# Linear attention into a soft mixture of experts: loads joined into longer rows, output chunks moved among the half-1 products

## The chip, the cores and the metric

The kernel runs on one core of a Trainium2 chip. The metric is device time in microseconds of one execution. Five engines work side by side, each through its own list of instructions in order: TensorE (PE in the profile; PEld is its loading of weights), VectorE (DVE), ScalarE (ACT), GpSimd (POOL) and SyncE (SP), which here only issues DMAs. They wait for each other by semaphores. Data comes from HBM into SBUF (128 partitions) and goes back by 16 DMA engines, which all queues share.

## The reference

```python
def _attn_ref(q, k, v, g_norm):                  # all (8, 8, 576, 64)
    kv = np.einsum('bhsd,bhse->bhde', k, v)
    out = np.einsum('bhsd,bhde->bhse', q, kv)
    rms = np.sqrt(np.mean(out * out, axis=-1, keepdims=True) + 1e-06)
    return (out / rms * g_norm).astype(np.float32)

def _moe_ref(x, phi, w1, w2):                    # x (4608, 512), phi (512, 32), w1 (8, 512, 1024), w2 (8, 1024, 512)
    logits = x @ phi
    d = softmax over the tokens of logits        # written out with max, exp and sum
    slot_input = (d.T @ x).reshape(E, S_per_e, D)
    for e in range(E):
        h = np.maximum(slot_input[e] @ w1[e], 0.0)
        slot_out[e] = h @ w2[e]
    c = softmax over the slots of logits
    return (c @ slot_out.reshape(n_slots, D)).astype(np.float32)
```

x is the attention's result, laid out as 4608 tokens by 512 (8 heads by 64). There are 8 experts with 4 slots each. Everything is float32: 62 MB come in and 9.4 MB go out.

## The kernel before

**Memory.** One tile, `arena`, holds 160 KB of every partition. What is loaded gets a place in it, counted in KB per partition: `KV_AT[b]` for the keys and values of batch b (18 KB), `Q_AT[g]` for the queries of batches 2g and 2g+1 (18 KB), `W_AT` for the sixteen weight units (16 KB each; `w1` 7 lies in `xall` instead, and `w2` 2 in two halves). Places are used again: a load into a place waits until the last reader of what lay there is done. Outputs are put together in the arena too.

**Loads.** All loads and stores are issued by SP, in program order, and run in one hardware queue. At the start (L107 to L119) the kernel issues kv0, the constants, q0 and kv1 in pieces, then kv2, q1 (8 KB), kv3, q1 (10 KB), kv4 and q2. A DMA's semaphore is taken by the eighth-next DMA, which waits for it. `loads_behind` (L122) issues kv5, kv6, q3, kv7 after token tile 9, four weight units after tile 18, three after 27, one after 31; the others are issued between the later stages (L519 to L521, L665 to L674).

**Token loop.** There are 36 tiles T of 128 tokens. Nine tiles make a group of two batches. `kv_step(b, i)` forms the products of keys and values of batch b in three steps, ahead of the first tile that needs them: for b from 2 up, steps 0, 1 and 2 come before the query products of the three tiles ahead of that batch's first tile, so batch 2 (first tile 9) starts ahead of tile 6, batch 4 ahead of tile 15. Each tile then has `products` (TensorE, query by block-diagonal key-value matrix `bd`), `square` and `evict` (ACT), mean squares and root (DVE, ACT), scaling (POOL), logits (DVE), and `group_sum`, the softmax-weighted sum of the tokens (TensorE). `fill` issues matmuls of zeros at the start and behind the loop, on TensorE, whose results nothing reads.

**Experts.** Behind the loop the slots' inputs are transposed, and `expert_h(e)` (weights w1) and `expert_y(e, hf)` (weights w2) run on TensorE. The output's columns are made in two halves `hf`. For experts 2 to 7 a w2 unit holds one half for two experts: units 2, 3, 4 serve half 0, units 5, 6, 7 half 1.

**Output.** `gather(hf)` copies the summed products out of PSUM, `mix(hf)` adds the four partial sums by one matmul and copies the result to `z`, and `output(hf, k, f)` makes one of six chunks of a half: eight matmuls (four for each of two PSUM tiles), a copy by ACT (L655), a copy by DVE (L657), and one store of 768 KB (L658). Half-1 outputs need every half-1 product; half-0 outputs need half 0 alone. TensorE follows the written order of L680 to L700.

Of the kernel before, what the change touches and what calls it, by code (L numbers as in the profile page):

```python
# [14 lines left out]
P = 128  # L15
B, H, S, D = 8, 8, 576, 64
NPAIR = H // 2
NS = 32
NE = 8
# [8 lines left out]
NX = 14  # L28
EARLY = (18, 2, 0)
LATE_FILL = (21, 5, 5, 2, 2)  # L30
TOK = 4608
UNIT = 4096
KB = 256
ARENA = 160 * KB
LATE = 6
KV_AT = (0, 36, 54, 90, 108, 0, 18, 36)
Q_AT = (18, 72, 142, 54)
W_AT = {
# [3 lines left out]
}  # L42
SCRATCH = 1024
EPS_RMS = 1e-6
# [3 lines left out]
@with_exitstack  # L48
def soft_moe_linear_attention(ctx: ExitStack, tc: tile.TileContext, kv_in, q_in, w1_in, w2_in, c_in, out):


    nc = tc.nc
# [11 lines left out]
    def place(at, n):  # L64
        return arena[:, at * KB : at * KB + n]

    def load_kv(b, g=None):
        lo, hi = (0, TOK) if g is None else (2304 * g, 2304 * g + 2304)
        nc.sync.dma_start(place(KV_AT[b], TOK)[:, lo:hi], kv_in[b, :, lo:hi])

    def load_q(g, half=None):
        lo, hi = {None: (0, TOK), 0: (0, 2048), 1: (2048, TOK)}[half]
        nc.sync.dma_start(place(Q_AT[g], TOK)[:, lo:hi], q_in[g, :, lo:hi])

# [13 lines left out]
    def homes(kind, u):  # L88
        at = W_AT[kind, u]
        if at is None:  # L90
            return [xflat[:, :UNIT]]
        return [place(a, UNIT // len(at)) for a in at]

    def load_w(kind, u):
        parts = homes(kind, u)
        n = UNIT // len(parts)
        for i, t in enumerate(parts):
            nc.sync.dma_start(t, (w1_in if kind == "w1" else w2_in)[u, :, i * n : i * n + n])

    def w_block(kind, u, i):  # L100
# [4 lines left out]


    load_kv(0, 0)  # L107
    nc.sync.dma_start(cst, c_in)
    load_kv(0, 1)
    load_q(0, 0)  # L110
    load_kv(1, 0)
    load_kv(1, 1)
    load_q(0, 1)
    load_kv(2)
    load_q(1, 0)
    load_kv(3)
    load_q(1, 1)
    load_kv(4)
    load_q(2)  # L119


    loads_behind = {  # L122
        9: lambda: (load_kv(5), load_kv(6), load_q(3), load_kv(7)),
        18: lambda: [load_w(k, e) for e in range(2) for k in ("w1", "w2")],
        27: lambda: [load_w("w1", e) for e in range(2, 5)],
        31: lambda: load_w("w1", 5),
    }
# [308 lines left out]

    fill(EARLY[0])

    for g in range(2):
        kv = Kv(0, "o" if g else "kv", 2 if g else None)  # L440
        kv.products(2 * g)
        kv.products(2 * g + 1)
        kv.borders((g,))
        kv.slots((g,))
        fill(EARLY[1 + g])
    T_at, diag_at, pb_at, d_at, sums_at = {}, {}, {}, {}, {}
# [70 lines left out]
    for i in todo_sums:  # L517
        group_sum(*i)
    load_w("w1", 6)  # L519
    load_w("w1", 7)  # L520
    load_w("w2", 2)  # L521
    fill(LATE_FILL[0], home=ps.tile([P, 512], F32, tag="m", name="fill"), cols=512)
# [88 lines left out]
    def expert_y(e, hf):  # L611
        u, at = w2_unit(e, hf)
        for c in range(8):
            j = c % 4
            nc.tensor.matmul(  # L615
                pY[32 * j : 32 * j + 32, hf, :256],
                lhsT=hTs[e][:, c],
                rhs=w_block("w2", u, at + c),
                start=e == 0 and c < 4,
                stop=e == NE - 1 and c >= 4,  # L620
            )
# [42 lines left out]
    expert_h(0)  # L664
    load_w("w2", 3)  # L665
    expert_h(1)
    halves(0)
    load_w("w2", 4)
    load_w("w2", 5)
    combine(0)  # L670
    expert_h(2)
    halves(1)
    load_w("w2", 6)
    load_w("w2", 7)  # L674
    combine(1)
# [7 lines left out]
    gather(0)  # L683
    expert_y(2, 1)
    mix(0)
    expert_y(3, 1)
    output(0, *chunks[0])
    output(0, *chunks[1])
    expert_y(4, 1)
    expert_y(5, 1)  # L690
    output(0, *chunks[2])
    output(0, *chunks[3])
    expert_y(6, 1)
    expert_y(7, 1)
    gather(1)
    output(0, *chunks[4])
    mix(1)
    output(0, *chunks[5])
    for k, f in chunks:
# [3 lines left out]
def build_program():  # L703
    import concourse.bacc as bacc

    nc = bacc.Bacc("TRN2", target_bir_lowering=False, num_devices=1, dynamic_dma_scratch_size=SCRATCH)
    shapes = {"kv": (B, P, TOK), "qt": (B // 2, P, TOK), "w1": (NE, P, UNIT), "w2": (NE, P, UNIT), "cs": (P, 129)}
    args = [nc.dram_tensor(f"in_{n}_dram", s, F32, kind="ExternalInput").ap() for n, s in shapes.items()]
    args.append(nc.dram_tensor("out_0_dram", (2, NCH, P, 2, 4 * CT * NS), F32, kind="ExternalOutput").ap())
    with tile.TileContext(nc, schedule_with_timeline_sim=True) as tc, tc.manual_schedule():  # L710
        soft_moe_linear_attention(tc, *args)
    return nc
# [43 lines left out]
```

## Time and profile before

| | |
|---|---|
| median of 3 runs | 176.16 us (176.01 to 177.61) |
| the profiled execution, its own time | 175.97 us |
| span of that execution in the profile | 174.2 us |
| PE busy | 148.2 us (85%) |
| DVE, ACT, POOL busy | 88.3, 86.8, 55.7 us |
| read from HBM, written | 61.93 MB, 9.44 MB |
| DMA packets | 6645, 71.68 MB, mean 411 GB/s |

The span runs from the first instruction to the last; the execution's own time holds what lies around it as well. Busy time of an engine is a mean over stages that have different limits, so the stages are read one by one: the token loop from about 12 to 103 us, the softmax's end to 116, the experts to 139, the outputs from 144. A row of the timeline gives start, length, engine, line, operation, output and inputs with shapes, the count of instructions in it, and in brackets how long the engine had stood idle before it and what released it. "DMA to landing" is the time from a DMA's issue to its semaphore.

### The profile page before, as it was taken

Reading aid. Unit: us, or ns where it says so; the run is one execution under the profiler, and the core shown is the slowest. Engines: PE = TensorE matmul, PEld = TensorE weight load, DVE = VectorE, ACT = ScalarE, POOL = GpSimd, SP = SyncE. Lnnn points to the kernel's source line nnn. Section 1 sums busy time; section 2 is a strip of 40 time slices with the busy share of each in tenths; the row PEclk is TensorE's granted clock in tenths of the full one; section 3 lists DMA queues with packets and bytes.
Section 4 is the critical chain, followed back from the end, with each engine's and each line's share of the span. In section 5 each row is a group of like instructions: output and inputs, shape, how many; then the busy total and the mean of one; then the engine's idle time right before and its main releaser. Section 6 shows DMA issues by size and latency. Waiting matters only on the chain.

```text
span 174.2 us, 4772 instructions
## 1 busy us (share of the span) xinstructions
PE 148.2 (85%) x2024; PEld 108.9 (63%) x2024; DVE 88.3 (51%) x180; ACT 86.8 (50%) x224; POOL 55.7 (32%) x65
## 2 busy tenths in 40 slices
PE   7577799999989899999999769989999959989500
PEld 5456778889779788888996555456556424445200
DVE  1122156566486565466663778733888114457600
ACT  2036286986957957878779553102234003336400
POOL 6000067656546676266773568000000000000000
PEclk9999999999999999999999999999999999999955
DMA  5999999999999999999999999999999999999994
GB/s 188 416 429 426 439 414 432 420 432 440 414 432 423 421 431 420 420 427 436 429 418 419 433 418 433 429 429 406 440 421 419 425 425 426 386 398 406 419 419 199
DMA packets 6645, 71.68 MB, mean 411 GB/s; under 512 B 736, under 2 KB 864, under 8 KB 2400
## 3 DMA queue, kind: packets, MB, share of 16 engines
q1 hardware_dynamic: 6624, 71.37, 97.5%
q8 instruction: 16, 0.26, 0.6%
q14 instruction: 5, 0.04, 0.1%
HBM read 61.93 MB, written 9.44 MB: 410 GB/s over the span
## 4 chain that ended last, share of the span: by engine, by line
PE 46%; DMA 20%; ACT 11%; DVE 11%; issue 3%; POOL 2%; SPq 1%; POOLq 0%; DVEq 0%
PE o L252 17%; DMA arena<-in_w_dram 11%; DMA arena<-in_kv_dram 9%; PE kvp_kv L184 8%; PE po L647 5%; PE pY L615 4%; PE ph L597 3%; DVE logits L329 3%; PE pS L386 2%; DVE ms L275 2%; ACT arena L655 2%; POOL part L324 2%; ACT bd L219 2%; PE o L243 2%; ACT sq L262 2%
## 5 line engine op out<-in xcount | busy, mean ns | idle before, releaser
L252 PE MATMUL o<-bd,arena 128*128 128x192 f32 x256 | 49.4, 336 | 1.4 <-ACT xall L270 0.6
L252 PEld LDWEIGHTS o<-bd,arena 128*128 128x128 f32 x256 | 40.8, 190 | 4.7 <-ACT xall L270 1.6
L302 POOL TENSOR_TENSOR xall<-xall,r 128x512 f32<-128x512 f32 x34 | 34.8, 1044 | 0.0
L324 POOL TENSOR_TENSOR part<-part,r 128x512 f32<-128x512 f32 x17 | 17.8, 1049 | 51.5 <-DVE r L293 51.5
L329 DVE TENSOR_REDUCE logits<-part 128x64 f32<-128x512 f32 (+1 forms) x19 | 19.3, 1015 | 16.1 <-POOL part L324 16.0
L275 DVE TENSOR_REDUCE ms<-sq 128x16 f32<-128x1024 f32 (+1 forms) x19 | 22.0, 1156 | 6.2 <-ACT sq L262 6.2
L262 ACT ACTIVATE sq<-o 128x512 f32<-128x512 f32 x36 | 21.5, 596 | 6.5 <-PE o L252 5.9
L270 ACT COPY xall<-o 128x512 f32<-128x512 f32 x34 | 20.6, 607 | 0.0
L184 PE MATMUL kvp_kv<-arena 128*64 128x64 f32 x480 | 17.3, 225 | 3.6 <-DMA arena<-in_kv_dram 3.6
L655 ACT COPY arena<-po 128x768 f32<-128x768 f32 x12 | 9.3, 800 | 20.2 <-DMA arena<-in_w_dram 10.3
L184 PEld LDWEIGHTS kvp_kv<-arena 128*64 128x64 f32 x480 | 15.2, 138 | 6.5 <-DMA arena<-in_kv_dram 4.5
L615 PE MATMUL pY<-arena,xall 128*32 128x256 f32 x256 | 15.2, 380 | 2.4 <-DMA arena<-in_w_dram 2.4
L657 DVE COPY arena<-po 128x768 f32<-128x768 f32 x12 | 11.3, 956 | 8.0 <-PE po L647 7.2
L647 PE MATMUL po<-logits,z 32*128 32x384 f32 x96 | 13.7, 526 | 1.6 <-ACT arena L655 1.0
L615 PEld LDWEIGHTS pY<-arena,xall 128*32 128x32 f32 x256 | 8.0, 110 | 9.1 <-issue 3.2
L597 PE MATMUL ph<-arena,sTe 128*32 128x256 f32 x224 | 12.7, 379 | 0.3 <-DVE sTe L544 0.3
L269 ACT COPY part<-o 128x256 f32<-128x256 f32 x34 | 12.6, 371 | 0.0
L386 PE MATMUL pS<-xall,d 128*32 128x129 f32 x288 | 10.7, 276 | 2.1 <-ACT d L374 2.1
L283 ACT ACTIVATE r<-ms,eps 128x16 f32<-128x16 f32 x17 | 5.2, 308 | 12.8 <-DVE ms L275 12.6
L647 PEld LDWEIGHTS po<-logits,z 32*128 32x128 f32 x96 | 6.3, 183 | 8.2 <-ACT arena L655 4.1
L291 DVE SCALAR_TENSOR_TENSOR r<-ms,r 128x16 f32<-128x16 f32 x17 | 3.0, 175 | 15.3 <-ACT r L284 15.3
L597 PEld LDWEIGHTS ph<-arena,sTe 128*32 128x32 f32 x224 | 7.2, 110 | 5.2 <-DVE sTe L544 0.6
(88 smaller groups left out, 143.9 us busy)
## 6 DMA issues: line engine op xcount, KB each, us to landing
arena<-in_w_dram SPq DMA_DIRECT2D x14, 2048.0 KB, 20.7
arena<-in_kv_dram SPq DMA_DIRECT2D x6, 2304.0 KB, 30.4
out_dram<-arena SPq DMA_DIRECT2D x12, 768.0 KB, 6.5
arena<-in_kv_dram SPq DMA_DIRECT2D x4, 1152.0 KB, 10.1
arena<-in_qt_dram SPq DMA_DIRECT2D x2, 2304.0 KB, 32.1
arena<-in_qt_dram SPq DMA_DIRECT2D x2, 1280.0 KB, 23.2
arena<-in_qt_dram SPq DMA_DIRECT2D x2, 1024.0 KB, 16.4
xall<-in_w_dram SPq DMA_DIRECT2D x1, 2048.0 KB, 15.4
```

The costliest lines, as they stand in the source:

```text
L184: nc.tensor.matmul(self.pkv[lo : lo + 64, w, g], lhsT=main[:, w, 1, c, lo : lo + 64], rhs=main[:, w, 0, c, lo : lo + 64], start=c == 0 and ...
L252: nc.tensor.matmul(o[:, r, :192], lhsT=q_main(2 * g + i)[:, r, at : at + P], rhs=bds[i][:, r], start=True, stop=True)
L262: nc.scalar.activation(sqs[s][:, T - starts[s]], o[:, :, 32:160], AF.Square, scale=0.125)
L270: nc.scalar.copy(xts[T % NX][:, :, :128], o[:, :, 32:160])
L275: nc.vector.tensor_reduce(out=mss[s], in_=sqs.pop(s).rearrange("p t j (w d) -> p (t j w) d", w=2), axis=AX.X, op=ALU.add)
L302: nc.gpsimd.tensor_tensor(out=x, in0=x, in1=r[:, i].rearrange("p (j w) -> p j w", w=2).unsqueeze(3).to_broadcast([P, 4, 2, D]), op=ALU.mult,)
L324: engine.tensor_tensor(out=part, in0=part, in1=rs_of[s].unsqueeze(3).to_broadcast([P, STAGES[s], H, NS]), op=ALU.mult)
L329: nc.vector.tensor_reduce(out=L[:, pos(starts[s]) : pos(starts[s]) + STAGES[s]], in_=parts.pop(s).rearrange("p t h n -> p t n h"), axis=AX ...
L386: nc.tensor.matmul(pS[32 * j : 32 * j + 32], lhsT=ds[G][:, i], rhs=x[:, j], start=i == 0, stop=i == GROUPS[G] - 1)
L597: nc.tensor.matmul(ph[32 * j : 32 * j + 32], lhsT=sTe[:, (4 * e + c) * NS : (4 * e + c + 1) * NS], rhs=w_block("w1", e, 4 * c + j), start= ...
L615: nc.tensor.matmul(pY[32 * j : 32 * j + 32, hf, :256], lhsT=hTs[e][:, c], rhs=w_block("w2", u, at + c), start=e == 0 and c < 4, stop=e == ...
L647: nc.tensor.matmul(po[:, u, : CT * NS].rearrange("p (g x) -> p g x", g=2), lhsT=z[lo : lo + 32, f * P : (f + 1) * P], rhs=cT[k][lo : lo + 32],
```

## The change

The places in the arena are laid out anew so that what is loaded one after the other lies side by side, and such loads become one DMA with a longer row per partition. The arrays in HBM are put together by the host to match.

- kv0, q0 and kv1 are loaded as before, in the same pieces and order (`load_head`).
- `t1`: kv2 and q1 in one row of 36 KB. It is issued at the start, in the place of kv2.
- kv3 alone (18 KB). It now lies where kv0 lay, and is issued behind the first batch's products in program order.
- `t2`: kv4, q2 and kv5 in one row of 54 KB, issued behind kv3.
- `t3`: kv6, q3 and kv7 in one row of 54 KB, after tile 9.
- Weight units w1 0 with w2 0, w1 1 with w2 1, w1 3 with w1 4 and w2 5 with w2 6 become rows of 32 KB; the other units stay single. The second pair is issued after tile 21 instead of 18.
- The fills at the start have 512 columns instead of 256, and half the count.
- At the end, half-0 chunks 0 and 1 stand ahead of the first two pending half-1 products, chunk 2 ahead of the next two, chunks 3 and 4 ahead of the last two, and chunk 5 between `gather(1)` and `mix(1)`.

```diff
-EARLY = (18, 2, 0)
+EARLY = (9, 1, 0)
...
-KV_AT = (0, 36, 54, 90, 108, 0, 18, 36)
-Q_AT = (18, 72, 142, 54)
+KV_AT = (0, 36, 54, 0, 90, 126, 18, 54)
+Q_AT = (18, 72, 108, 36)
 W_AT = {
-    ("w1", 0): (72,), ("w2", 0): (88,), ("w1", 1): (104,), ("w2", 1): (120,), ("w1", 2): (136,),
-    ("w1", 3): (0,), ("w1", 4): (16,), ("w1", 5): (32,), ("w1", 6): (48,), ("w1", 7): None,
-    ("w2", 2): (64, 152), ("w2", 3): (72,), ("w2", 4): (88,), ("w2", 5): (104,), ("w2", 6): (120,), ("w2", 7): (136,),
+    ("w1", 0): (72,), ("w2", 0): (88,), ("w1", 1): (128,), ("w2", 1): (144,), ("w1", 2): (104,),
+    ("w1", 3): (0,), ("w1", 4): (16,), ("w1", 5): (56,), ("w1", 6): (40,), ("w1", 7): None,
+    ("w2", 2): (32, 120), ("w2", 3): (72,), ("w2", 4): (88,), ("w2", 5): (128,), ("w2", 6): (144,), ("w2", 7): (104,),
 }
+W_ROWS = (2, 2, 1, 2, 1, 1, 1, 1, 1, 1, 2, 1)
+W_ORDER = [("w1", 0), ("w2", 0), ("w1", 1), ("w2", 1)] + [("w1", e) for e in range(2, NE)] + [("w2", u) for u in range(2, NE)]
...
+    def load_head(u, lo, hi):
+        at = (KV_AT[0], KV_AT[1], Q_AT[0])[u]
+        nc.sync.dma_start(place(at, TOK)[:, lo:hi], head_in[u, :, lo:hi])
+
+    def load_row(at, src):
+        nc.sync.dma_start(place(at, src.shape[-1]), src)
...
-    def load_w(kind, u):
-        parts = homes(kind, u)
-        n = UNIT // len(parts)
+    def load_w(*units):
+        lo = W_ORDER.index(units[0])
+        n = UNIT * len(units)
+        row = w_in[:, lo * UNIT * P : (lo * UNIT * P) + n * P].rearrange("o (p n) -> (o p) n", p=P)
+        parts = homes(*units[0])
+        if len(units) > 1:
+            parts = [place(W_AT[units[0]][0], n)]
         for i, t in enumerate(parts):
-            nc.sync.dma_start(t, (w1_in if kind == "w1" else w2_in)[u, :, i * n : i * n + n])
+            m = n // len(parts)
+            nc.sync.dma_start(t, row[:, i * m : i * m + m])
...
-    load_kv(0, 0)
+    load_head(0, 0, 2304)
     nc.sync.dma_start(cst, c_in)
-    load_kv(0, 1)
-    load_q(0, 0)
-    load_kv(1, 0)
-    load_kv(1, 1)
-    load_q(0, 1)
-    load_kv(2)
-    load_q(1, 0)
-    load_kv(3)
-    load_q(1, 1)
-    load_kv(4)
-    load_q(2)
+    load_head(0, 2304, TOK)
+    load_head(2, 0, 2048)
+    load_head(1, 0, 2304)
+    load_head(1, 2304, TOK)
+    load_head(2, 2048, TOK)
+    load_row(KV_AT[2], t1_in)
...
     loads_behind = {
-        9: lambda: (load_kv(5), load_kv(6), load_q(3), load_kv(7)),
-        18: lambda: [load_w(k, e) for e in range(2) for k in ("w1", "w2")],
-        27: lambda: [load_w("w1", e) for e in range(2, 5)],
-        31: lambda: load_w("w1", 5),
+        9: lambda: load_row(KV_AT[6], t3_in),
+        18: lambda: load_w(("w1", 0), ("w2", 0)),
+        21: lambda: load_w(("w1", 1), ("w2", 1)),
+        27: lambda: (load_w(("w1", 2)), load_w(("w1", 3), ("w1", 4))),
+        31: lambda: load_w(("w1", 5)),
     }
...
-    fill(EARLY[0])
+    fill(EARLY[0], cols=512)
...
-        fill(EARLY[1 + g])
+        fill(EARLY[1 + g], cols=512)
+    load_row(KV_AT[3], kv3_in)
+    load_row(KV_AT[4], t2_in)
...
     halves(0)
-    load_w("w2", 4)
-    load_w("w2", 5)
+    load_w(("w2", 4))
     combine(0)
     expert_h(2)
     halves(1)
-    load_w("w2", 6)
-    load_w("w2", 7)
+    load_w(("w2", 5), ("w2", 6))
+    load_w(("w2", 7))
...
     gather(0)
-    expert_y(2, 1)
     mix(0)
-    expert_y(3, 1)
     output(0, *chunks[0])
     output(0, *chunks[1])
+    expert_y(2, 1)
+    expert_y(3, 1)
+    output(0, *chunks[2])
     expert_y(4, 1)
     expert_y(5, 1)
-    output(0, *chunks[2])
     output(0, *chunks[3])
+    output(0, *chunks[4])
     expert_y(6, 1)
     expert_y(7, 1)
     gather(1)
-    output(0, *chunks[4])
+    output(0, *chunks[5])
     mix(1)
-    output(0, *chunks[5])
     for k, f in chunks:
         output(1, k, f)
...
+        "in_t1_dram": np.concatenate([kv[2], qm[1]], axis=1),
+        "in_kv3_dram": kv[3],
+        "in_t2_dram": np.concatenate([kv[4], qm[2], kv[5]], axis=1),
+        "in_t3_dram": np.concatenate([kv[6], qm[3], kv[7]], axis=1),
+        "in_w_dram": np.concatenate(rows)[None],
```

More of the change, by code (lines that the diff above doesn't have):

```diff
@@ L48, in soft_moe_linear_attention @@
 @with_exitstack
-def soft_moe_linear_attention(ctx: ExitStack, tc: tile.TileContext, kv_in, q_in, w1_in, w2_in, c_in, out):
+def soft_moe_linear_attention(ctx: ExitStack, tc: tile.TileContext, head_in, t1_in, kv3_in, t2_in, t3_in, w_in, c_in, out):
     nc = tc.nc
@@ L65, in place @@
         return arena[:, at * KB : at * KB + n]
[L67 to L73, printed above, removed]
+    def load_head(u, lo, hi):
[3 more added lines that the diff above has]
+        nc.sync.dma_start(place(at, src.shape[-1]), src)
     def kv_main(b, g):
@@ L518, in soft_moe_linear_attention @@
         group_sum(*i)
-    load_w("w1", 6)
-    load_w("w1", 7)
-    load_w("w2", 2)
+    load_w(("w1", 6))
+    load_w(("w1", 7))
+    load_w(("w2", 2))
     fill(LATE_FILL[0], home=ps.tile([P, 512], F32, tag="m", name="fill"), cols=512)
@@ L664, in soft_moe_linear_attention @@
     expert_h(0)
-    load_w("w2", 3)
+    load_w(("w2", 3))
     expert_h(1)
     halves(0)
-    load_w("w2", 4)
-    load_w("w2", 5)
+    load_w(("w2", 4))
     combine(0)
@@ L706, in build_program @@
     nc = bacc.Bacc("TRN2", target_bir_lowering=False, num_devices=1, dynamic_dma_scratch_size=SCRATCH)
-    shapes = {"kv": (B, P, TOK), "qt": (B // 2, P, TOK), "w1": (NE, P, UNIT), "w2": (NE, P, UNIT), "cs": (P, 129)}
+    shapes = {
+        "head": (3, P, TOK), "t1": (P, 2 * TOK), "kv3": (P, TOK), "t2": (P, 3 * TOK), "t3": (P, 3 * TOK),
+        "w": (1, 2 * NE * P * UNIT), "cs": (P, 129),
+    }
     args = [nc.dram_tensor(f"in_{n}_dram", s, F32, kind="ExternalInput").ap() for n, s in shapes.items()]
@@ L743 @@
     cs = np.concatenate([ph, np.concatenate([g_norm, g_norm])[:, None]], axis=1)
-    arrays = {
-        "in_kv_dram": kv.reshape(B, P, TOK),
-        "in_qt_dram": qm,
-        "in_w1_dram": np.ascontiguousarray(w1),
-        "in_w2_dram": np.ascontiguousarray(w2),
+    kv = kv.reshape(B, P, TOK)
+    w = {("w1", e): w1[e] for e in range(NE)} | {("w2", u): w2[u] for u in range(NE)}
+    rows, u = [], 0
+    for n in W_ROWS:
+        rows.append(np.concatenate([w[k] for k in W_ORDER[u : u + n]], axis=1).reshape(-1))
+        u += n
+    arrays = {
+        "in_head_dram": np.stack([kv[0], kv[1], qm[0]]),
+        "in_t1_dram": np.concatenate([kv[2], qm[1]], axis=1),
[3 more added lines that the diff above has]
+        "in_w_dram": np.concatenate(rows)[None],
         "in_cs_dram": np.ascontiguousarray(cs),
```

## The prediction

> **What bounds the kernel now.** I read the page's header first, then the windows by stage, then the timeline where one stage hands over to the next. Windows rows: stretch, length, then busy time (x instructions) of PE, PEld, DVE, ACT and POOL, granted clock, DMA share, GB/s.
>
> ```profile
> span 174.2 us, 4772 instructions
> ```
> ```profile
> 27.00:103.00 76.00, 73.82 (x1023) 63.05 (x1022) 46.60 (x91) 57.52 (x160) 45.79 (x45) 1.00 1.01 427
> 116.40:139.10 22.70, 22.64 (x416) 13.40 (x416) 13.04 (x32) 5.22 (x11) 0.00 (x0) 1.00 1.01 422
> 147.00:158.00 11.00, 10.24 (x114) 5.11 (x106) 5.69 (x8) 3.80 (x5) 0.00 (x0) 1.00 0.96 395
> ```
>
> Two things are full at once. The DMA is busy from the first microseconds to the end, at 422 to 427 GB/s, and a little less (0.96) where the outputs begin. TensorE is full too in the token loop: 73.82 of the 76 us from 27 to 103, so whatever delays it there comes back with at most 2.2 us recovered. The end belongs to the DMA: the last output store is issued at 164.7 and lands 8.5 later, at 173.2, and 1.0 us after that the span ends.
>
> ```profile
> L658 SPq DMA_DIRECT2D out_dram<-arena x1: 644/644/644, 164.7 to 164.7; - x1
> ...
> DMA to landing us min/median/max: 8.5/8.5/8.5
> ```
>
> So the last stores wait in a queue behind others: compute is ahead of the stores at the end. That lead is what a delay of compute has to eat first, and I work it out below.
>
> **Fewer, longer rows.** Loads other than the constants go from 33 to 23 DMAs, the bytes stay. In rows per DMA engine (128 partitions over 16 engines, 8 rows a DMA) 80 rows go. The nearest rows for the price of a row are the stores' 6 KB rows and the loads' 10 to 18 KB rows:
>
> ```profile
> 20.00:72.00 52.00, 50.67 (x671) 43.45 (x672) 30.91 (x60) 40.11 (x112) 30.53 (x30) 1.00 1.01 426
> 160.00:171.00 11.00, 3.44 (x24) 1.42 (x20) 3.67 (x4) 2.91 (x4) 0.00 (x0) 0.72 1.01 420
> ```
>
> An engine moves 6144 B in 6144x16/420 = 234 ns and 18432 B in 692 ns; the straight line through both leaves 5 ns for a row without bytes. 80 x 5 ns = 0.4 us off the DMA's time (ends: 0 if the 420 is due to stores being stores, 0.8 if a row costs double that; no row here is longer than 18 KB, so a loss of the same 0.4 isn't excluded). This is the whole gain of the joining, if the DMA stays the bound.
>
> **What the joining makes later.** A joined load has one landing for all it holds. kv2 and q1 are now one load, t1; kv4, q2 and kv5 are t2; kv6, q3 and kv7 are t3. kv2 before is issued at 4.5 and lands 22.4 later, at 26.9, and TensorE takes it at once:
>
> ```profile
> L69 SPq DMA_DIRECT2D arena<-in_kv_dram x1: 495/495/495, 4.5 to 4.5; - x1
> ...
> DMA to landing us min/median/max: 22.4/22.4/22.4
> ```
> ```profile
> 27.02 1.01 PEld L184 LDWEIGHTS kvp_kv<-arena 128*64 128x64 f32 x32 [0.23 <-DMA arena<-in_kv_dram]
> 27.03 1.15 PE L184 MATMUL kvp_kv<-arena 128*64 128x64 f32 x32
> ...
> 50.27 1.15 PE L184 MATMUL kvp_kv<-arena 128*64 128x64 f32 x32
> ```
>
> The row at 27 is step 0 of batch 2, ahead of tile 6 (the one at 50.3 is batch 4's). It waited 0.23 us for that landing, so it has no slack. The queue ahead of t1 is unchanged (kv0, q0, kv1 in the same six pieces), so t1 lands later than kv2 by the time of q1's 2304 KB: 2.36 MB at 427 GB/s = 5.5 us, at 32.4. TensorE runs in program order, so tiles 6 and up, and ACT, DVE and POOL behind them, start 5.4 us later. t2 lands 72 KB a partition (9.44 MB, 22.1 us) behind t1, at 54.5, where batch 4's products come at 50.3 before and 55.7 after: no second wait. t3 lands where kv7 did, near 71, for batch 6, nine tiles behind batch 4: nothing. kv3, now loaded into kv0's place, is issued once kv0's products are done, with t1 queued until 32: nothing.
>
> From 27 on the shift X = 5.4 holds, less up to 0.5 (half a microsecond of ACT waits that might close; I take 0).
>
> The loads behind the loop wait on SP for TensorE's reads and move by X too. Their slack is the queue still to run: the tightest is the w2 unit 3, issued after the first expert.
>
> ```profile
> L98 SPq DMA_DIRECT2D arena<-in_w_dram x1: 327/327/327, 118.4 to 118.4; - x1
> ...
> DMA to landing us min/median/max: 13.2/13.2/13.2
> ```
>
> It lands at 131.6, of which its own 2.1 MB at 422 GB/s are 5.0: the queue before it runs until about 126.6, 8.2 us after its issue. At X = 5.4 the issue is 2.8 us ahead still. Costed at nothing; above X of about 7 (8.2 less the 1.2 that an issue takes, below) the DMA runs dry here.
>
> **The output stage.** The experts' chain (22.64 of 22.7 busy) passes X on, and the last half-0 product ends at E = 133.68 + 5.36 + X = 139.04 + X. From there the new order is output chunk by chunk; its pieces are in the timeline of before:
>
> ```profile
> 133.68 5.36 PE L615 MATMUL pY<-arena,xall 128*32 128x256 f32 x96
> 141.48 1.07 PE L615 MATMUL pY<-arena,xall 128*32 128x256 f32 x16 [2.44 <-DMA arena<-in_w_dram]
> 142.48 0.70 PE L635 MATMUL pz<-y,sel 128*128 128x256 f32 x2
> 144.11 1.56 PE L647 MATMUL po<-logits,z 32*128 32x384 f32 x12
> 146.77 1.93 PE L615 MATMUL pY<-arena,xall 128*32 128x256 f32 x32
> 148.63 1.56 PE L647 MATMUL po<-logits,z 32*128 32x384 f32 x12
> 153.15 0.93 PE L647 MATMUL po<-logits,z 32*128 32x384 f32 x8
> 154.01 0.70 PE L635 MATMUL pz<-y,sel 128*128 128x256 f32 x2
> ```
> ```profile
> 139.11 0.42 DVE L631 COPY y<-pY 128x256 f32<-128x256 f32 x1 [3.83 <-PE pY L615]
> 143.22 0.43 DVE L637 COPY z<-pz 128x256 f32<-128x256 f32 x1 [3.68 <-PE pz L635]
> 153.29 0.42 DVE L631 COPY y<-pY 128x256 f32<-128x256 f32 x1 [0.93 <-PE pY L615]
> ```
> ```profile
> 146.15 19.23 SPq L658 DMA_DIRECT2D out_dram<-arena  x12
> ```
>
> Gather ends at E + 0.49; pz starts 0.3 later (153.71 to 154.01) and is 0.70 long; z 0.47; 0.3 again to the first chunk: E + 2.26. In before a product pair stood between gather and mix and hid them; in the new order nothing does, but that pair also waited 2.44 us for its weights, which have landed now. Two chunks take 2.66 (144.11 to 146.77), a product pair 1.86 (146.77 to 148.63), one chunk 0.75 before the next work can start. Chunks 0 and 1, pair, chunk 2, pair, chunks 3 and 4, pair: 2.26 + 2.66 + 1.86 + 0.75 + 1.86 + 2.66 + 1.86 = E + 13.9. Then chunk 5, whose last copy, DVE's, ends 2.0 later (just ahead of its store: 144.11 to 146.15) at 15.9; z of half 1 behind that copy to 16.3, chunk 6 at 16.6, and its store 2.04 behind: E + 18.6 = 157.6 + X. The pieces are measured; their new order is good to about 0.7.
>
> No store of half 1 can go before that. Six stores of 786 KB at 420 GB/s are 6 x 1.87 = 11.2 us, and the first needs some time from issue to first byte. The nearest row is the very first load's:
>
> ```profile
> L69 SPq DMA_DIRECT2D arena<-in_kv_dram x1: 371/371/371, 0.7 to 0.7; - x1
> ...
> DMA to landing us min/median/max: 5.5/5.5/5.5
> ```
>
> Its 1.18 MB at 426 GB/s are 2.8 of the 5.5 us, which leaves 2.7; the ends are 0 and 2.7. I take 1.2, below the middle, as the queue is awake by then. The last landing is then not before 157.6 + X + 12.4 = 170.0 + X. The DMA's own end is 173.2 - 0.4 = 172.8. So up to X = 2.8 compute is hidden and the change gains 0.4; beyond, each microsecond counts in full. X = 5.4 gives 175.4 for the landing.
>
> **The clock.** TensorE now stands still for 5.4 us at tile 6. Rows of PE alone (stretch, length, busy, granted clock, DMA share, GB/s):
>
> ```profile
> 137.43:140.85 3.42, 1.61 (x32) 1.00 1.01 426
> 161.33:164.74 3.41, 2.15 (x18) 1.00 1.02 423
> 164.74:168.15 3.41, 0.00 (x0) 0.50 1.01 418
> ```
> ```profile
> 1.05 3.71 PE L429 MATMUL fill<-zeros 128*128 128x256 bf16 x18 [1.05 <-DVE zeros L136]
> ...
> 109.67 1.24 PE L429 MATMUL fill<-zeros 128*128 128x512 bf16 x5
> ```
>
> The stretch with half its time busy keeps 1.00; the empty one is at 0.50. A gap of 5.4 us leaves at least 2.7 of some 3.4 us stretch empty, which is nearer to the empty row. Half clock is not free: the first fills took 206 ns for 256 columns, later ones 124 (248 for 512), so the spell at the start lasted nearly the 3.7 us of the fills. After the restart a spell of the same kind loses half its length, at most 1.9 us; 0 if the clock holds. I take 1.2, as the restart falls somewhere inside a stretch. So X = 6.6, under the 7 of the dry queue.
>
> The Trainium skill, "TensorE: Matmul & The Clock Gate", Part 1, says that one idle window of about 3.4 us, free-running, halves the clock. By that rule 5.4 us of idle contain a whole window in (5.4 - 3.4)/3.4 = 59% of placements, an estimate; the drop after the row with 2.15 us busy speaks for less idle being enough.
>
> **The sum.** Landing 170.0 + 6.6 = 176.6, span + 1.0 = 177.6. The profiled execution took 175.97 for a span of 174.2, 1.8 more, so 179.4; the median of the runs, 176.16, is 0.2 above it: 179.6. The other fills (9 of 512 columns for 18 of 256) move the same columns and cost nothing.
>
> **The rivals.**
> - The clock holds. For it, the row at 1.00 with half its time empty; against it, that more is empty here. 178.4.
> - Not slower: the late t1 is absorbed before chunk 6, so X there is under 2.8 and the DMA's queue still sets the end: 176.16 - 0.4 = 175.8, at best 175.3. For it, the 2.2 us that TensorE idles in the loop and the chunks sent ahead; against it, 5.4 less 2.2 is still 3.2, and those idles are waits in the same chain. It decides below X = 2.8.
> - Dry queue: X above 7 (a clock spell of 1.9 or a second late landing, t2 for batch 4 with under 1.2 us to spare). Then w2 arrives late as well, and half-1 products wait: 181 to 183.
> - Faster: longer rows gain more than 5 ns each and the 0.96 stretch closes (0.4 us): 174.3 or below. The DMA share of 1.01 nearly everywhere leaves no room.
>
> **How the numbers follow.** Forecast (late t1 and a clock spell) 0.43, 178.6 to 180.8; clock holds 0.25, 177.4 to 179.2; absorbed 0.20, 175.3 to 177; dry queue 0.07; faster 0.05. The range from 175.4 to 180.8 leaves out the last two and a little of the absorbed case, under 2 in 10. A measurement of this kernel tells about 1% from no change: below 174.4 is faster, above 177.9 slower. Slower: 0.43 + 0.07 + four fifths of 0.25, 0.69, rounded to 0.68; same: the rest of the clock case and the absorbed case, 0.26; faster 0.06.
>
> **What would show it.** Right: a wait of the kv products on the t1 load of some 5 us at tile 6, at 32; clock below 1.00 in the stretch behind it; the loop's end near 109 instead of 103; half-0 products ending near 145; stretches of DMA share well under 0.96 between 150 and 165; the first half-1 store issued near 164. Wrong: kv products of batch 2 starting before 30, or the loop ending at 103 to 105, or DMA share at 1.0 through the output stage with an end at 172.8. Also wrong is the row price, if stretches of 54 KB rows move less than 426 or over 430 GB/s.

## The result and the profile after

The changed kernel takes 182.33 us (median of 6 runs, 181.5 to 183.35) beside 176.83 us for the kernel before on the same chip (6 runs, 176.01 to 177.70): a ratio of 1.031, 95% interval 1.026 to 1.037. It is slower, as forecast, but by 2.7 us more than forecast, and outside the range given. The profiled execution took 182.17 us, for a span of 180.3; predicted was a span of 177.6.

From the page of the changed kernel: its span, then the granted clock and the DMA's share in 40 slices of 4.5 us.

```profile
span 180.3 us, 4735 instructions
...
PEclk9999998599999999999999999999999999999975
DMA  6999999999999999999889997999999999998993
```

There is one notch in the clock, in slices 7 and 8 (from 27 us on), and several in the DMA's row, behind the middle. TensorE's timeline of the changed kernel has what lies in the notch, and where the loop ends:

```profile
32.42 1.98 PE L186 MATMUL kvp_kv<-arena 128*64 128x64 f32 x32 [5.59 <-DMA arena<-in_t_dram]
34.33 2.72 PE L254 MATMUL o<-bd,arena 128*128 128x192 f32 x8
...
108.88 1.55 PE L254 MATMUL o<-bd,arena 128*128 128x192 f32 x8
```

Batch 2's products wait 5.59 us for t1 and start at 32.42, 5.4 later than before. They and the eight products behind them run long: 1.98 us for what takes 1.15, and 2.72 for what takes 1.55 at the loop's end. The last tile's products start at 108.88, where the kernel before has them at 101.50 (its row stands further down, in the table): a shift X of 7.4 us. The windows cut where the clock changes (stretch, length, busy time of PE, PEld, DVE, ACT and POOL, granted clock, DMA share, GB/s):

```profile
26.46:29.87 3.41, 0.37 (x3) 0.07 (x1) 2.15 (x4) 2.19 (x6) 2.94 (x3) 1.00 0.85 362
29.87:33.28 3.41, 0.85 (x16) 0.86 (x18) 1.49 (x5) 0.52 (x2) 1.86 (x3) 0.50 1.00 422
33.28:36.70 3.42, 3.42 (x29) 3.30 (x26) 0.87 (x2) 0.00 (x0) 1.30 (x2) 0.50 1.18 507
36.70:40.10 3.40, 3.40 (x61) 3.02 (x61) 0.00 (x0) 1.77 (x5) 0.00 (x0) 1.00 1.15 499
```

The half clock lasts two stretches of 3.41 us. TensorE works in it from 32.42 to 36.70, 4.3 us, and half of that is lost: 2.1 us, which with the 5.4 makes X to a tenth.

Late in the loop and behind it the DMA runs dry at times. These are windows of the changed kernel, then of the kernel before, over the same stretches:

```profile
84.00:92.00 8.00, 8.00 (x128) 6.79 (x124) 4.55 (x12) 7.15 (x20) 4.41 (x5) 1.00 0.86 321
...
106.00:114.00 8.00, 5.69 (x73) 4.74 (x72) 5.74 (x17) 5.24 (x16) 5.54 (x6) 1.00 0.83 309
...
124.00:132.00 8.00, 8.00 (x152) 4.81 (x148) 3.77 (x10) 1.97 (x4) 0.00 (x0) 1.00 0.96 369
...
158.00:168.00 10.00, 8.50 (x82) 3.81 (x78) 5.92 (x8) 3.84 (x6) 0.00 (x0) 1.00 0.91 372
```
```profile
84.00:92.00 8.00, 8.00 (x122) 7.41 (x124) 5.28 (x8) 5.64 (x17) 5.38 (x6) 1.00 1.01 426
...
106.00:114.00 8.00, 7.44 (x73) 3.71 (x65) 6.53 (x15) 1.30 (x5) 2.05 (x3) 1.00 1.01 428
...
124.00:132.00 8.00, 8.00 (x156) 4.83 (x152) 6.53 (x15) 2.19 (x6) 0.00 (x0) 1.00 1.01 422
...
158.00:168.00 10.00, 5.08 (x38) 2.24 (x32) 5.30 (x6) 4.00 (x5) 0.00 (x0) 0.84 1.01 418
```

Against the rates of before the four stretches lose 8 x (1 - 321/426) = 2.0, 2.2, 1.0 and 1.1 us of DMA time, 6.3 in all, about what the span grew by (6.1). That sum is tempting and, as the experiments show, it is not the reason: nothing on TensorE waits for what comes late in the first three of them. The end hangs on the first half-1 store. Its issue and the last store's, each with the time to its landing:

```profile
L662 SPq DMA_DIRECT2D out_dram<-arena x1: 332/332/332, 164.8 to 164.8; - x1
...
DMA to landing us min/median/max: 5.2/5.2/5.2
```
```profile
L662 SPq DMA_DIRECT2D out_dram<-arena x1: 751/751/751, 171.2 to 171.2; - x1
...
DMA to landing us min/median/max: 8.1/8.1/8.1
```

The first is issued at 164.8, which is 157.6 + X less 0.2: the chain of TensorE was forecast well. The last lands at 179.3, 14.5 later, where the prediction had 12.4. The windows of the changed kernel behind that issue say why:

```profile
164.80:168.00 3.20, 2.84 (x24) 1.21 (x22) 2.29 (x3) 1.71 (x3) 0.00 (x0) 1.00 0.90 358
168.00:172.00 4.00, 2.07 (x14) 0.82 (x12) 2.32 (x3) 1.87 (x3) 0.00 (x0) 1.00 1.01 413
172.00:176.00 4.00, 0.00 (x0) 0.00 (x0) 0.00 (x0) 0.00 (x0) 0.00 (x0) 0.65 1.02 419
176.00:179.30 3.30, 0.00 (x0) 0.00 (x0) 0.00 (x0) 0.00 (x0) 0.00 (x0) 0.50 0.38 155
```

Length by rate, they move 5.0 MB: the six stores (4.7) and 0.3 left of earlier ones. All of it at 420 GB/s would take 11.9 us. The first stretch, with the queue nearly empty, loses 3.2 x (1 - 358/420) = 0.5. The last moves 0.51 MB, 1.2 us of work for sixteen engines, in 3.3: some engines are done and the slowest is not, which costs 2.1. A landing is that of the slowest engine (the last section of this document has the row: over the last 2.3 us the engines' mean busy share is 0.12, two of sixteen on average).

### The profile page after: what moved, and what is told of

Its sections match the earlier page's. It is cut to its first block, busy times and chain, and to the rows that moved or that the text cites. A ratio compares the mean times of both kernels' runs of the same rounds, so it can differ in the third digit from the quotient of the medians.

```text
span 180.3 us, 4735 instructions
## 1 busy us (share of the span) xinstructions
PE 151.9 (84%) x2014; PEld 110.6 (61%) x2014; DVE 88.3 (49%) x180; ACT 87.0 (48%) x224; POOL 55.7 (31%) x65
## 4 chain that ended last, share of the span: by engine, by line
PE 41%; DMA 27%; DVE 11%; ACT 8%; issue 2%; SPq 2%; POOL 2%; POOLq 0%; DVEq 0%
DMA arena<-in_t_dram 15%; PE o L254 15%; DMA arena<-in_w_dram 10%; PE kvp_kv L186 8%; PE pY L619 5%; PE po L651 3%; PE ph L601 3%; DVE logits L331 3%; DVE arena L661 2%; PE pS L388 2%; DVE ms L277 2%; DMA out_dram<-arena 2%; POOL part L326 2%; SPq L71 2%; ACT bd L221 1%
## 5 line engine op out<-in xcount | busy, mean ns | idle before, releaser
L254 PE MATMUL o<-bd,arena 128*128 128x192 f32 x256 | 50.4, 341 | 1.9 <-ACT bd L231 0.8
L254 PEld LDWEIGHTS o<-bd,arena 128*128 128x128 f32 x256 | 41.9, 194 | 5.0 <-ACT xall L272 1.6
L326 POOL TENSOR_TENSOR part<-part,r 128x512 f32<-128x512 f32 x17 | 17.8, 1049 | 58.8 <-DVE r L295 58.8
L264 ACT ACTIVATE sq<-o 128x512 f32<-128x512 f32 x36 | 21.5, 596 | 14.3 <-PE o L254 13.9
L186 PE MATMUL kvp_kv<-arena 128*64 128x64 f32 x480 | 18.7, 237 | 6.8 <-DMA arena<-in_t_dram 5.6
L186 PEld LDWEIGHTS kvp_kv<-arena 128*64 128x64 f32 x480 | 16.7, 149 | 10.3 <-DMA arena<-in_t_dram 5.9
L651 PEld LDWEIGHTS po<-logits,z 32*128 32x128 f32 x96 | 5.8, 183 | 9.4 <-ACT arena L659 5.0
L431 PE MATMUL fill<-zeros 128*128 128x512 bf16 x31 | 9.4, 461 | 1.1 <-DVE zeros L138 1.1
```

The lines of the kernel that those rows point to most:

```text
L186: nc.tensor.matmul(self.pkv[lo : lo + 64, w, g], lhsT=main[:, w, 1, c, lo : lo + 64], rhs=main[:, w, 0, c, lo : lo + 64], start=c == 0 and ...
L254: nc.tensor.matmul(o[:, r, :192], lhsT=q_main(2 * g + i)[:, r, at : at + P], rhs=bds[i][:, r], start=True, stop=True)
L264: nc.scalar.activation(sqs[s][:, T - starts[s]], o[:, :, 32:160], AF.Square, scale=0.125)
L326: engine.tensor_tensor(out=part, in0=part, in1=rs_of[s].unsqueeze(3).to_broadcast([P, STAGES[s], H, NS]), op=ALU.mult)
L651: nc.tensor.matmul(po[:, u, : CT * NS].rearrange("p (g x) -> p g x", g=2), lhsT=z[lo : lo + 32, f * P : (f + 1) * P], rhs=cT[k][lo : lo + 32],
```

## The experiments

What was to be told apart: that late landings hold TensorE up, and the first half-1 store is late with it; that the DMA's dry queue costs by itself; and that the new order, the new places or the longer rows cost something. The table has, for every kernel, the start of the last tile's products (T35), the issue of the first half-1 store (S), the last landing (Z), from the timelines and the rows of DMA issues, all in us, and the ratio to the kernel before.

| kernel | T35 | S | S - T35 | Z - S | span | ratio (95%) |
|---|---|---|---|---|---|---|
| before | 101.5 | 158.8 | 57.3 | 14.4 | 174.2 | 1 |
| changed | 108.9 | 164.8 | 55.9 | 14.5 | 180.3 | 1.031 (1.026 to 1.037) |
| t1 in two | 107.2 | 162.9 | 55.7 | 14.0 | 177.9 | 1.015 (1.009 to 1.021) |
| before with t1 | 109.0 | 165.2 | 56.2 | 14.4 | 180.8 | 1.028 (1.022 to 1.034) |
| before with the new order | 101.4 | 157.7 | 56.3 | 15.7 | 174.3 | 0.994 (0.991 to 0.997) |
| changed, TensorE kept busy | 107.0 | 162.7 | 55.7 | 14.4 | 178.2 | 1.019 (1.011 to 1.026) |
| before, held up by 5 us | 106.6 | 162.0 | 55.4 | 13.4 | 176.4 | 1.010 (1.004 to 1.016) |
| before, held up by 7 us | 108.8 | 164.2 | 55.4 | 13.7 | 178.8 | 1.022 (1.016 to 1.028) |
| changed, old order | 108.9 | 171.1 | 62.2 | 14.6 | 186.8 | 1.061 (1.054 to 1.068) |
| the same, w2 5 and 6 apart | 109.7 | 165.1 | 55.4 | 14.5 | 180.7 | 1.032 (1.026 to 1.038) |
| t1 and t2 in two | 103.1 | 159.3 | 56.2 | 13.9 | 174.1 | 0.997 (0.993 to 1.000) |
| the same, kv3 earlier | 101.7 | 161.1 | 59.5 | 14.3 | 176.3 | 1.006 (1.002 to 1.009) |
| the same, w2 5 and 6 apart | 101.4 | 157.2 | 55.9 | 15.7 | 173.8 | 0.997 (0.993 to 1.000) |
| before, another execution | 101.9 | 160.7 | 58.8 | 14.5 | 176.1 | one run |

The columns S - T35 and Z - S carry the case. S follows T35 by 55.4 to 56.3 us in every kernel but four, and in those four TensorE waited for a weight in the output stage. Z follows S by 13.4 to 14.6 in every kernel but two, and those two are the ones where S is earliest (157.2 and 157.7) and the DMA's queue, not TensorE, sets the end, at 172.9 and 173.4.

**t1 in two.** Alone kv2 should come when it used to.

```diff
-    load_row(KV_AT[2], t1_in)
+    load_row(KV_AT[2], t1_in[:, :TOK])
+    load_row(Q_AT[1], t1_in[:, TOK:])
```

> The changed kernel with kv2 and q1 as two loads of 18 KB rows again, all else as changed. Theory (the late landing of t1 carries the loss): kv2's products start at 27, the clock stays at 1.00, no window of the loop under 1.0 of DMA share, ratio to the kernel before 0.99 to 1.005. Rival (long rows, the new places or the new order cost by themselves): ratio 1.015 to 1.03 although tile 6 is on time.

Half the loss went (1.015), not all of it: the theory's range is missed, and the ratio lies at the lower edge of the rival's, for a reason that neither named. Batch 2 is in time now (its products start at 27.7), and the wait stands at batch 4 instead, whose keys and values lie in t2. The timeline and the windows of this kernel:

```profile
54.60 1.98 PE L187 MATMUL kvp_kv<-arena 128*64 128x64 f32 x32 [2.67 <-DMA arena<-in_t_dram]
```
```profile
50.79:54.20 3.41, 0.87 (x24) 1.00 0.95 405
54.20:57.61 3.41, 3.01 (x35) 0.51 0.86 373
```

(The windows show PE alone.) In the changed kernel nothing waits for t2, because TensorE is already behind by then: the second late landing was hidden by the first. Here the wait costs its 2.7 us and half of a stretch at half clock besides.

**t1 alone, in the kernel before.** The converse: the old arena, order and loads, with kv2 and q1 in one row.

```diff
-    load_kv(2)
-    load_q(1, 0)
-    load_kv(3)
-    load_q(1, 1)
+    nc.sync.dma_start(place(KV_AT[2], 2 * TOK), t1_in)
+    load_kv(3)
```

> The kernel before with one edit, kv2 and q1 in one load. Theory: kv2's products wait until 32.4, the clock falls for a spell, the loop ends near 110.5 and the ratio is 1.02 to 1.035, all or nearly all of the change's loss. Rival (the loss comes from the other joins or from the order): ratio under 1.01.

1.028 of the 1.031, with the 5.28 us wait at 32.57 and the same half clock. This one join is enough for nearly the whole loss.

**t1 and t2 in two.** Both late landings undone; all else of the change stays.

```diff
-    load_row(KV_AT[2], t1_in)
+    load_row(KV_AT[2], t1_in[:, :TOK])
+    load_row(Q_AT[1], t1_in[:, TOK:])
...
-    load_row(KV_AT[4], t2_in)
+    load_row(KV_AT[4], t2_in[:, :TOK])
+    load_row(Q_AT[2], t2_in[:, TOK:])
```

> The changed kernel with kv2 apart from q1 and kv4 apart from q2 and kv5, so that neither batch's keys and values wait for their neighbours; t3, the rows of two weight units, the places and the order stay. Theory: tiles 6 and 15 are on time, clock 1.00 behind the start, DMA share 1.00 or more from 84 to 132, ratio 0.99 to 1.0. Rival (the weights' rows and places or t3 cost too): ratio 1.005 or more, with the queue dry somewhere behind the loop.

The ratio is 0.997 (0.993 to 1.000), and the clock stays at 1.00. Together the two landings are the whole loss, within the noise. A smaller one shows now: 0.87 us of waiting for kv3 at 38.3, which the kernel before loaded ahead of the second part of q1 and this one behind all of it.

**The shift by itself.** To see what a hold-up of TensorE costs without any joined load, matmuls of zeros whose results nothing reads were put ahead of tile 6, 24 and 33 of 512 columns, in the kernel before; and 24 in the changed kernel, where they fill the wait for t1 and keep the clock up.

```diff
+        if T == 6:
+            fill(24, home=ps.tile([P, 512], F32, tag="m", name="fill"), cols=512)
         for b in range(1, B):
```

> The changed kernel with 24 fills of 512 columns on TensorE while it waits for t1 (24 x 0.224 = 5.4 us). Theory: products of batch 2 start at 32.4 as in the changed kernel, the clock stays at 1.00, the shift at the loop's end is 5.4 instead of 7.4, the queue doesn't run dry behind it, and the ratio is 1.008 to 1.018. Rival (the clock's fall costs nothing that counts, the late landing alone makes the loss): ratio 1.027 to 1.035 as in the changed kernel.

> The kernel before, its loads untouched, with 24 fills of 512 columns (5.4 us) on TensorE ahead of batch 2's products. Theory (the shift of compute makes the loss, whatever causes it): tiles from 6 on are 5.4 us late, the loads behind the loop come so late that the DMA loses some of its lead there, ratio 1.008 to 1.018. Rival (the loss is made by joined rows and places, the shift is covered by the DMA's queue): ratio 1.00 to 1.005.

> The same with 33 fills (7.4 us, the whole shift of the changed kernel). Theory: each further microsecond counts in full, 2.0 us over the run with 24 fills, ratio 1.022 to 1.033, as for the changed kernel and for t1 alone. Rival: ratio under 1.01.

In the changed kernel the clock holds (the stretches from 29.87 to 36.70 are granted 1.00), T35 comes 1.9 us earlier and the span is 2.1 us shorter: that is the price of the half clock. The ratio, 1.019, lies just above the 1.008 to 1.018 expected, and the queue does run short behind this shift, which was not expected. In the kernel before, hold-ups of 5.1 and 7.3 us lengthen the span by 2.2 and 4.6; between them 2.1 us of shift cost 2.4, so there each microsecond counts in full. Now the dry queue. Windows of the changed kernel with fills, then of before with 24, then of before with 33:

```profile
106.00:114.00 8.00, 6.28 (x76) 4.61 (x75) 6.62 (x15) 3.76 (x13) 5.94 (x6) 1.00 0.88 328
...
124.00:132.00 8.00, 8.00 (x156) 4.81 (x148) 5.50 (x12) 1.91 (x4) 0.00 (x0) 1.00 0.95 376
```
```profile
106.00:114.00 8.00, 6.28 (x76) 4.40 (x75) 6.59 (x17) 3.43 (x12) 5.60 (x6) 1.00 1.01 408
124.00:132.00 8.00, 8.00 (x156) 4.83 (x152) 5.55 (x12) 1.83 (x5) 0.00 (x0) 1.00 0.99 378
```
```profile
106.00:114.00 8.00, 5.70 (x73) 4.71 (x73) 5.82 (x17) 5.11 (x15) 5.67 (x6) 1.00 0.92 350
124.00:132.00 8.00, 8.00 (x156) 4.83 (x152) 3.77 (x10) 1.97 (x4) 0.00 (x0) 1.00 0.98 387
```

The queue runs short at a shift of 5.1 already, where the prediction said 7. And it costs nothing by itself: S - T35 is 55.4 in both kernels with a plain hold-up, though they lose DMA time at 106 to 114 in unlike amounts, and 55.9 both in the changed kernel, which loses 6.3 us of DMA time, and in the last kernel of the series, which loses little. So the dry queue is not the reason. The changed kernel's late weights have a margin left, a small one, as the issue of the last unit and TensorE's timeline show:

```profile
L104 SPq DMA_DIRECT2D arena<-in_w_dram x1: 468/468/468, 133.1 to 133.1; - x1
...
DMA to landing us min/median/max: 23.9/23.9/23.9
```
```profile
158.41 1.93 PE L619 MATMUL pY<-arena,xall 128*32 128x256 f32 x32
```

It lands at 157.0, and its products start at 158.4 without a wait.

**The order of the chunks.** Alone, in the kernel before, and undone, in the changed one; the lines are those of the change's diff.

> The kernel before with the new order of chunks and half-1 products alone. Theory: the DMA queue sets the end, last landing near 173, ratio 0.995 to 1.005. Rival (the order costs, as mix is no longer hidden behind a product): ratio 1.01 to 1.02 with DMA share under 0.95 after 150.

> The changed kernel with the order of chunks and half-1 products of the kernel before. Theory (the order is a small matter beside the shift): ratio 1.027 to 1.037. Rival (the new order makes up for a part of the shift, or adds to it): above 1.04, or under 1.022.

Alone the new order gives 0.994, the DMA's share in 147 to 158 is 1.00 instead of 0.96, and S is 1.1 us earlier. Undone in the changed kernel it costs 5.7 us more (182.33 to 188.02), where I had expected a small difference; the rival had "above 1.04", but no cause for it. Timeline and windows of that kernel:

```profile
151.70 1.93 PE L619 MATMUL pY<-arena,xall 128*32 128x256 f32 x16 [5.22 <-DMA arena<-in_w_dram]
153.56 1.22 PE L639 MATMUL pz<-y,sel 128*128 128x256 f32 x2
```
```profile
148.00:158.00 10.00, 6.30 (x46) 2.47 (x46) 0.94 (x2) 0.57 (x1) 0.00 (x0) 0.66 0.51 216
```

w2 5 and 6 are one load, and w2 5 is needed first: ahead of `mix` in the old order, so that every chunk of half 0 stands behind the wait. Half the DMA's time in those 10 us goes unused. In the new order the products of half 0 end at 146.4 and the first ones with w2 5 start at 151.2: 4.7 us of other work stand ahead of them. To see that it is this join:

```diff
-W_ROWS = (2, 2, 1, 2, 1, 1, 1, 1, 1, 1, 2, 1)
+W_ROWS = (2, 2, 1, 2, 1, 1, 1, 1, 1, 1, 1, 1, 1)
...
-    load_w(("w2", 5), ("w2", 6))
+    load_w(("w2", 5))
+    load_w(("w2", 6))
```

> The changed kernel with the old order of chunks and half-1 products and with w2 units 5 and 6 as two loads. Theory (the 1.06 of the old order comes from unit 5 landing 5 us later with unit 6, in front of mix and every chunk): the first half-1 product waits no more than 1 us, ratio 1.025 to 1.037 as for t1 alone. Rival (the new order is what counts, whatever the weights do): ratio stays above 1.05.

1.032 with the old order, as in the changed kernel with the new one. In the execution profiled the clock fell once more, at 18 us, so that T35 is 0.8 later; S - T35, 55.4, is 0.5 shorter than in the changed kernel. So the new order makes good what the join of w2 5 and 6 costs, and little else here.

**kv3 in time as well.** From the kernel with t1 and t2 in two, q1 is cut and kv3 put ahead of its second piece.

```diff
-    load_row(Q_AT[1], t1_in[:, TOK:])
+    load_row(Q_AT[1], t1_in[:, TOK : TOK + 2048])
...
     load_row(KV_AT[3], kv3_in)
+    nc.sync.dma_start(place(Q_AT[1], TOK)[:, 2048:], t1_in[:, TOK + 2048 :])
```

> The changed kernel with kv2, a first piece of q1, kv3, the rest of q1, kv4 and then q2 with kv5 as loads of their own, in the order of the kernel before; t3, the weights' rows, the places and the new order of chunks stay. Theory: with batch 3's keys and values ahead of q1's second piece again, tile 10 loses its 0.9 us wait, the loop ends at 103 or before, and the ratio is 0.990 to 0.996: the order's own 0.994, and at most 0.4 us more from the joins that are left. Rival (the joins that are left cost something): ratio above 0.997.

The loop ends on time (T35 101.7), and the kernel, which was expected at 0.990 to 0.996, is slower for it: 1.006 (1.002 to 1.009). TensorE now reaches the half-1 products early enough to wait for w2 5 and 6, even in the new order. Timeline and windows of this kernel:

```profile
145.85 3.59 PE L622 MATMUL pY<-arena,xall 128*32 128x256 f32 x32 [2.00 <-DMA arena<-in_w_dram]
```
```profile
142.39:145.80 3.41, 1.21 (x6) 0.30 (x4) 1.66 (x2) 1.19 (x2) 0.00 (x0) 1.00 0.94 404
145.80:149.21 3.41, 3.36 (x32) 1.39 (x32) 0.00 (x0) 0.00 (x0) 0.00 (x0) 0.51 0.98 415
```

Two microseconds of waiting and 1.7 at half clock (3.59 us for products that take 1.93): S comes 3.7 late. Eight of the twelve executions took 177.9 us or more, like the one profiled, and four 176.1 to 176.7; the difference is about what the half clock costs, but no profile of one of the four was taken. That is the third late landing that an earlier one had hidden. With w2 5 and 6 apart too (the diff above):

> The changed kernel with every load apart whose first part is needed before its last: kv2 and the first piece of q1 ahead of kv3, kv4 apart from q2 with kv5, and w2 5 apart from w2 6. The new order of chunks stays, and so do kv6 with q3 and kv7, and the joined units of w1 and w2 0, 1 and of w1 3 with 4. Theory: the whole loss of the change is landings that come after their first consumer, and no join gains anything by itself, as the queue is full either way; so nothing is late here, no product waits over 1 us for a load behind tile 6, the granted clock is 1.00 behind the start, and the ratio is that of the new order alone: 0.990 to 0.997. Rival A: the new places of the loads cost something of their own (the unit w1 6 waits for the last tile's products): the DMA share is under 0.97 in 106:114 us and the ratio is 0.998 or more. Rival B: the joins that stay gain as well: the ratio is under 0.990.

Median 175.79 us, ratio 0.997 (0.993 to 1.000), S at 157.2, no wait over 1 us for a load behind tile 6 and a DMA share of 1.00 in 106 to 114. That is what the theory expected, with every join gone whose first part is needed before its last. The longer rows that stay move a little more. Windows of the same stretch of the token loop, of this kernel and then of before with the new order:

```profile
27.00:72.00 45.00, 43.95 (x626) 37.84 (x627) 27.59 (x52) 34.38 (x96) 27.45 (x27) 1.00 1.01 431
```
```profile
27.00:72.00 45.00, 43.94 (x626) 37.85 (x627) 27.54 (x52) 34.37 (x96) 27.46 (x27) 1.00 1.01 427
```

45 x 4/427 = 0.4 us, and its span is 0.5 shorter than that of the kernel below it. But the ratios of these two, 0.997 and 0.994, cannot be told apart, so which of them is the best version stays open. The Trainium skill, "DMA: Bandwidth & Descriptors", section "Rules for kernel authors", asks for at least 1 MiB in a DMA; the loads that were joined were of 1 to 2.25 MiB each, and joining them further is worth what these rows show, at most.

**The kernel before, once more.** Its runs fall into two groups: beside the kernel with the new order 5 of 17 lie at 175.8 to 176.0 us and 12 at 177.4 to 177.7, while all 12 of the new order lie at 175.8 to 176.2.

> The kernel before, unchanged, for a second profile of it. Its executions fall into two groups, near 175.9 and near 177.5 us. If the group is made by the output stage, a profile of the slower one shows stores issued later or a lower DMA share after 147 than the profile at hand; if by the loads, a later landing of the last weights than 151.

This execution, at 177.9 us, is of the upper group. Its windows, then one of the profiled execution of before that the prediction read:

```profile
139.10:142.51 3.41, 0.99 (x21) 0.50 (x16) 0.42 (x1) 0.00 (x0) 0.00 (x0) 0.99 1.00 428
142.51:145.92 3.41, 3.41 (x26) 1.09 (x18) 0.42 (x1) 0.00 (x0) 0.00 (x0) 0.50 1.00 428
```
```profile
140.85:144.26 3.41, 2.78 (x38) 1.36 (x42) 0.43 (x1) 0.00 (x0) 0.00 (x0) 1.00 1.02 432
```

Both have the same wait of 2.4 us for w2 5. In the lower execution it is cut by the border of two stretches, which are 1.61 us (the prediction's row from 137.43) and 2.78 us busy, and the clock holds. In the upper one it falls into a single stretch, 0.99 us of it are busy, and the next is at 0.50: S comes 1.9 us later. The new order fills that wait with work, and in the kernel before with that order the upper group is gone. One profile of each kind shows it.

Two things limit this. In the last kernel of the series, which has the new order too, 2 of 12 executions lie at 177.1 and 177.3, and no profile of one was taken. And the ratios in the table depend on how many executions of before fell into the lower group. These were 5 of 17 beside the kernels with t1 in two, t1 alone, the new order alone and TensorE kept busy; 6 beside the hold-ups, the old order and t1 and t2 in two; 12 beside the old order with w2 5 and 6 apart and beside kv3 earlier; and 9 beside the last of the series. That alone moves the mean of before between 177.1 and 176.5 us, 0.4%. Against the lower group only (mean 175.95) the new order (mean 176.03) gains nothing: its 0.994 is the upper group that is gone.

## Why the prediction was wrong

**Right: the late t1.** 5.4 us at tile 6, at 32.4, to the tenth. It passes through loop and experts undiminished; the half-0 products end at 141.08 + 5.36 = 146.4, which is 139.04 + 7.4.

**Right: the output stage.** The first half-1 store 18.6 us behind the half-0 products was forecast, 18.3 came. Each microsecond beyond the threshold counts in full, as the two hold-ups show.

**The step that failed: "Six stores of 786 KB at 420 GB/s are 6 x 1.87 = 11.2 us, and the first needs some time from issue to first byte. ... I take 1.2".** From the first half-1 store's issue to the last landing it takes 14.5 us, not 12.4, and more than the 13.9 that even the upper end of 2.7 would have given. The start cost 0.5, what was left of earlier stores 0.7, and 2.1 went to something that had no term: the sixteen engines don't finish together. The row was there: in the kernel before the first half-1 store was issued at 158.8 and the last landed at 173.2, 14.4 later. All kernels here that wait for TensorE take 13.4 to 14.6. In before 1.8 us of it were earlier stores (380 GB/s over those 14.4 us are 5.47 MB, 0.75 more than the six stores), so it is made up differently there. With it, the threshold comes out at X = 1 and not 2.8 (157.4 + X + 14.4 against a landing at 172.9), with the 13.4 of the shorter hold-up at 2; so before was closer to being bound by TensorE than "compute is ahead of the stores" made it. This term put the forecast out of its range: with its 2.1 us alone the forecast would have been 181.7, and with the clock's 0.8 alone 180.4.

**Mis-sized: the clock.** The mechanism was right and the spell fell as forecast; it was put at 1.2 us with an upper end of 1.9, and measured 2.0. A spell of two stretches had not been thought of. 2.1 + 0.8 - 0.2 (the store came a little early) = 2.7, the whole difference between the spans of 180.3 and 177.6. By the rule of the Trainium skill, "TensorE: Matmul & The Clock Gate", Part 1, a drop takes one whole idle window of about 3.4 us, and the clock comes back after a busy one. The trace agrees with the second half, as the busy stretch from 33.28 to 36.70 ends the spell; of the first half it shows less to be enough: in the changed kernel the two stretches that were each followed by one at half clock were not empty (0.37 and 0.85 us busy), and in the kernel with t1 in two the wait was 2.7 us.

**Wrong in its limit, right in its price: "above X of about 7 the DMA runs dry here".** It ran short at 5.1. The 8.2 us of slack came from a landing as well, that of the slowest engine. By bytes, w2 unit 3 was issued when 51.7 MB had been asked for (392 KB a partition, the constants and what the instruction queues read), and the windows from 0 to the issue show what had been moved:

```profile
0.00:118.40 118.40, 106.98 (x1452) 87.00 (x1456) 62.61 (x135) 72.30 (x201) 55.71 (x65) 1.00 0.99 417
```

417 x 118.4 = 49.4 MB: 2.3 MB were left, 5.5 us and not 8.2. Nor was this the only gate to look at: the first two notches of the DMA stand where w1 units 2 and 6 are issued, at 88.6 and 110.5. "Costed at nothing" held all the same. The rival of the dry queue gave 181 to 183, and 182.3 came; it was still not the reason, since the half-1 products that it had waiting did not wait.

**Right, in part for a reason not given: "no second wait", "nothing" for kv3, and no price for w2 5 and 6.** Each of the three is late by itself, by 2.7, 0.9 and 2.0 us, and was covered by the shift of t1. For t2 the prediction reckoned with that (batch 4 at 55.7 instead of 50.3); for kv3 and w2 it did not, and that they cost nothing was luck. In the changed kernel they cost nothing; they surfaced one after another as the earlier ones were undone.

**The row price.** 0.4 us was forecast for all the joins, and the one pair of windows above gives 0.4 for 45 us alone. Its 431 GB/s is just over the 430 that the prediction named as the sign of a wrong price (430 to 432 as the window is cut), so a row was priced somewhat low. The gain is hidden wherever TensorE sets the end.

## What to carry to other kernels

Join two loads only if the first consumer of the joined row needs the last byte of it anyway, or can wait for it; where the queue is full and the rows are already 10 to 18 KB, the joined row gains a percent of the rate at best, and the first part lands later by the whole time of the second. When a late landing is undone, look for the next one that it had hidden, and move independent work (here finished output chunks) into the wait that can't be undone. Read a slack from bytes asked for and bytes moved, and an end from a whole measured chain, here from the issue of the first store to the last landing: a landing is that of the slowest engine.

## What the hardware showed that was not expected

The clock falls with less idle time than a whole stretch of 3.41 us. Stretches in which TensorE was busy for 0.37, 0.85, 0.87, 0.99 and 1.21 us were followed by one at half clock; those with 1.61 and 2.78 us were not. Busy time alone doesn't decide it, though. The prediction's stretch from 161.33, busy for 2.15 us, was followed by an empty one at 0.50. Early in two other kernels, a stretch with 1.74 us lost the clock and one with 1.52 us kept it (PE alone; the changed kernel with TensorE kept busy, then the last kernel of the series):

```profile
5.02:8.43 3.41, 1.74 (x43) 1.00 0.99 408
8.43:11.84 3.41, 3.30 (x44) 0.50 1.02 432
```
```profile
3.76:7.18 3.42, 1.52 (x30) 1.00 1.02 413
7.18:10.59 3.41, 2.56 (x62) 1.00 1.01 426
```

What else counts stays open. Where the border of the stretches falls differs from execution to execution, so one and the same wait of 2.4 us cost 1.9 us more in one profiled execution of before than in the other.

At the end of the stores the slowest DMA engine is 2.1 us behind the mean in the changed kernel. In the kernel before, the stretch from 171.0 to the last landing shows the same at a smaller size:

```profile
171.00:173.20 2.20, 0.00 (x0) 0.00 (x0) 0.00 (x0) 0.00 (x0) 0.00 (x0) 0.50 0.42 176
```

It moves 0.39 MB, 0.9 us of work at 420 GB/s, in 2.2. Here too lies why Z - S is 13.4 in one kernel and 14.5 in another. The end of the changed kernel, then the whole stretch from S to the last landing in before with 24 fills:

```profile
177.00:179.30 2.30, 0.00 (x0) 0.00 (x0) 0.00 (x0) 0.00 (x0) 0.00 (x0) 0.50 0.12 48
```
```profile
162.00:174.20 12.20, 4.69 (x32) 2.23 (x32) 4.58 (x5) 3.39 (x5) 0.00 (x0) 0.80 1.02 418
174.20:175.40 1.20, 0.00 (x0) 0.00 (x0) 0.00 (x0) 0.00 (x0) 0.00 (x0) 0.50 0.29 118
```

With 24 fills 5.2 MB are moved from S on, 0.2 more than in the changed kernel, and the engines still run full until 1.2 us before the end; in the changed kernel a few run alone for the last 2.3. Why they come apart by such unlike amounts stays open.
